# A gated linear attention with a maxout expert on one Trainium2 core: engine orders written out operation by operation, steps skewed by one tile, and the q and k products split over two engines

## The chip, the cores and the metric

The kernel runs on one core of a Trainium2 chip. The metric is the device time of one execution in microseconds (us); lower is better. A profiled execution also gives a span, from its first to its last instruction, and a trace of every engine: PE (TensorE; PEld is its weight loads), DVE (VectorE), ACT (ScalarE), POOL (GpSimd) and SP (SyncE, which issues all the transfers here).

## What is computed

Per batch (4) and head (8) a state of 48 x 48 is carried along 768 positions, decayed by a sigmoid gate; its output, with the heads side by side, goes through a maxout expert.

```python
f = 1.0 / (1.0 + np.exp(-f_logit))
for t in range(S):
    state = f[:, :, t, :, None] * state + np.einsum('bhd,bhe->bhde', k[:, :, t], v[:, :, t])
    y[:, :, t] = np.einsum('bhd,bhde->bhe', q[:, :, t], state)
x = y.transpose(0, 2, 1, 3).reshape(B * S, H * D)       # 3072 x 384
out = np.maximum(x @ w1, x @ w2) @ w_out                # 384 -> 1024 -> 384
```

## The kernel before

The 768 positions are cut into 6 chunks of 128 and every chunk is taken for the 4 batches in turn: 24 tiles, tile i being chunk i // 4 of batch i % 4, with 128 positions on the partitions and 8 heads x 48 on the free axis. Since max(a, b) = b + relu(a - b), the expert is computed as x (w2 w_out) + relu(x (w1 - w2)) w_out: `wd` = w1 - w2 and `w2o` = w2 w_out are made once at the start (24 transposes `w2tp` and 24 matmuls `w2op`).

One tile goes through these steps, each named by the tile that it writes:

- load: `ft`, `kt`, `qt`, `vt`, 192 KB each, one DMA each on SP (L63).
- `e`, `ell` on ACT (L177, L178): the log of the gate, negated; `vb` on DVE (L184): v in bf16.
- `cum` on PE (L191, L193): its sums along the chunk, as a matmul with a triangle of ones, and four small matmuls for the sum of the whole chunk.
- `ei`, `ed`, `fl` on ACT (L199 to L201): the exponentials of these; `kp` = k times `ei` and `qp` = q times `ed` on POOL (L203, L205; `qp` of tile 0 on DVE).
- `tr` on PE (L214): eight transposes of `kp` and `qp`; `trs` on DVE (L218) takes them out of PSUM.
- `a` on PE (L229): the eight 128 x 128 products of q and k; `am` on DVE (L232) masks them.
- `sa` on PE (L244), `tmp` on DVE (L248), two `st` on POOL (L251): the new state, for the same batch's next chunk, four tiles later. The last chunk needs none.
- `y` on PE (L256, L261): eight matmuls with `am`, and four with the old state except in the first chunk; `x` on ACT (L264).
- `xtp` on PE (L271; three transposes) and `xT` on DVE (L273).
- `d` on PE, two halves of 12 matmuls (L150), `gT` on ACT, the relu, one for each half (L152); `o` on PE, 11 matmuls (L162), written as six and five; `ob` on DVE (L167); the store of 192 KB on SP (L169).

No scheduler reorders anything: each engine, SP too, runs its instructions in the order in which the program writes them. The order is one of whole steps. Tiles 0 and 1 go through the attention steps, then the weights are prepared, then tiles 2 to 5 are begun; from i = 2 a loop writes `s_cum(i+3)`, `s_y(i)`, `u_d(i-1, 0)`, `s_tr(i+2)`, `u_d(i-1, 1)`, `s_xT(i)`, `s_a(i+1)`, `u_o(i-1, ...)`, `s_ell(i+4)`, `s_v(i+4)`, `load(i+6)`. So a tile is begun four steps ahead of its `y`, and every engine finds the instructions of one step in that order. On SP the loads of tiles 0 and 1 come first, then all weights (six of 512 KB, two of 768 KB), then tiles 2 to 5; later each step has one store and four loads.

PSUM has three buffers for `cum`, `sa`, `y`, `tr` and `xtp` (tag "s"), three for `d`, `o` and the weights (tag "mm"), one for `a`.

Of the kernel before, what the change touches and what calls it, by code (L numbers as in the profile page):

```python
# [14 lines left out]

@with_exitstack
def kernel(
# [35 lines left out]
    ld = {}  # L55

    def load(i):
        c, b = divmod(i, B)
        sl = slice(c * C, (c + 1) * C)
        t = {}  # L60
        for name, src in (("f", f_logit), ("k", k), ("q", q), ("v", v)):
            t[name] = loads.tile([C, H, D], F32, name=f"{name}t", tag=f"{name}t")
            nc.sync.dma_start(out=t[name], in_=src[b, :, sl, :].rearrange("h p d -> p h d"))  # L63
        ld[i] = t

    w1_f = consts.tile([C, JG, d_ff], F32, name="w1_f")
    w2_f = consts.tile([C, JG, d_ff], F32, name="w2_f")
    wo_f = consts.tile([C, FG, dm], F32, name="wo_f")

    def load_w(dst, src, j, n=1):  # L70
        nc.sync.dma_start(out=dst[:, j:j + n, :],
                          in_=src[j * C:(j + n) * C, :].rearrange("(j p) x -> p j x", p=C))

    load(0)
    load(1)
    for j in range(JG):
        load_w(w2_f, moe_w2, j)
    for j in range(0, FG, 4):
        load_w(wo_f, moe_w_out, j, 4)
    for j in range(JG):  # L80
        load_w(w1_f, moe_w1, j)
    load(2)
    load(3)
    load(4)
    load(5)


# [9 lines left out]
    for t in ell_b:  # L97
        nc.vector.memset(t, 0.0)
    nc.vector.memset(ones_col, 1.0)
    make_upper_triangular(nc, ut, 1.0, diag=True)  # L100
    make_identity(nc, ident)
    for t in kp_b + qp_b:
        nc.vector.memset(t, 0.0)
    nc.vector.tensor_copy(mask, ut.unsqueeze(1).to_broadcast([C, H, C]))
    for b in range(B):
        for t in st_b[b]:
            nc.vector.memset(t, 0.0)


# [6 lines left out]
    def u_w2_cast(j):  # L116
        nc.vector.tensor_copy(w2_h[:, j, :], w2_f[:, j, :])

    def u_wo_cast(h):
        s = slice(h * 2, h * 2 + 2)  # L120
        nc.scalar.copy(wo[:, s, :], wo_f[:, s, :])

    def u_wd(j):
        nc.vector.tensor_sub(wd[:, j, :], w1_f[:, j, :], w2_f[:, j, :])

    def u_w2T(f):
        ps = ps_m.tile([C, JG, C], BF16, name="w2tp", tag="mm")
        for j in range(JG):
            nc.tensor.transpose(out=ps[:, j, :], in_=w2_h[:, j, f * C:(f + 1) * C], identity=ident)  # L129
        nc.vector.tensor_copy(w2T[:, f, :], ps.rearrange("p j c -> p (j c)"))  # L130

    def u_w2o(j):
# [4 lines left out]
        nc.scalar.copy(w2o[:, j, :], ps)  # L137


    st = {}  # L140

    def u_d(i, half):
        s = st[i]
        if half == 0:
            s["g"] = work.tile([C, FG, C], BF16, name="gT", tag="gT")
        ps = ps_m.tile([C, 4, C], F32, name="d", tag="mm")
        for n in range(4):
            f = half * 4 + n
            for j in range(JG):
                nc.tensor.matmul(out=ps[:, n, :], lhsT=wd[:, j, f * C:(f + 1) * C], rhs=s["xT"][:, j, :],  # L150
                                 start=(j == 0), stop=(j == JG - 1))
        nc.scalar.activation(s["g"][:, half * 4:half * 4 + 4, :], ps, AF.Relu)  # L152

    def u_o(i, half):
        s = st[i]
        if half == 0:
            s["o"] = ps_m.tile([C, dm], F32, name="o", tag="mm")
        mms = [(s["xT"][:, j, :], w2o[:, j, :]) for j in range(JG)]
        mms += [(s["g"][:, f, :], wo[:, f, :]) for f in range(FG)]
        cut = 6  # L160
        for n in (range(0, cut) if half == 0 else range(cut, len(mms))):
            nc.tensor.matmul(out=s["o"], lhsT=mms[n][0], rhs=mms[n][1],  # L162
                             start=(n == 0), stop=(n == len(mms) - 1))
        if half == 1:
            c, b = divmod(i, B)
            ob = work.tile([C, dm], F32, name="ob", tag="ob", bufs=5)
            nc.vector.tensor_copy(ob, s["o"])  # L167
            r0 = b * S + c * C
            nc.sync.dma_start(out=out[r0:r0 + C, :], in_=ob)  # L169
            del st[i]  # L170


    def s_ell(i):
        t = ld[i]
        e = work.tile([C, dm], F32, name="e", tag="e")
        ell = ell_b[i % 2]
        nc.scalar.activation(e, t["f"].rearrange("p h d -> p (h d)"), AF.Exp, scale=-1.0)  # L177
        nc.scalar.activation(ell[:, :, 0:D], e.rearrange("p (h d) -> p h d", h=H), AF.Ln, bias=1.0)  # L178
        st[i] = {"ell": ell}

    def s_v(i):
        t = ld[i]
        vb = work.tile([C, dm], BF16, name="vb", tag="vb", bufs=6)
        nc.vector.tensor_copy(vb, t["v"].rearrange("p h d -> p (h d)"))  # L184
        st[i]["v"] = vb

    def s_cum(i):
        s, t = st[i], ld[i]
        ell = s["ell"]
        ps = ps_s.tile([C, 512], F32, name="cum", tag="s")  # L190
        nc.tensor.matmul(out=ps[:, 0:dm], lhsT=ut, rhs=ell[:, :, 0:D], start=True, stop=True)  # L191
# [11 lines left out]
        nc.gpsimd.tensor_mul(kp[:, :, 0:D], t["k"], ei.rearrange("p (h d) -> p h d", h=H))  # L203
# [1 line left out]
        eng.tensor_mul(qp[:, :, 0:D], t["q"], ed.rearrange("p (h d) -> p h d", h=H))  # L205
        s.update(fl=fl, qp=qp, kp=kp)
        del ld[i]

    def s_tr(i):
# [7 lines left out]
        tr = work.tile([C, 2, NP, C], BF16, name="trs", tag="trs", bufs=3)  # L217
        nc.vector.tensor_copy(tr, ps)  # L218
        s["tr"] = tr

    def s_a(i):
# [10 lines left out]
        nc.vector.tensor_mul(am.rearrange("p o n c -> p (o n) c"),  # L232
                             ps.rearrange("p o n c -> p (o n) c"), mask)
        s["am"] = am

    def s_y(i):
# [3 lines left out]
        old, new = st_b[b][c % 2], st_b[b][(c + 1) % 2]  # L240
        if c < nch - 1:
            sa = ps_s.tile([C, NP, 2 * D], F32, name="sa", tag="s")
            for p in range(NP):
                nc.tensor.matmul(out=sa[:, p, :],  # L244
                                 lhsT=s["kp"][:, 2 * p:2 * p + 2, :].rearrange("p h d -> p (h d)"),
                                 rhs=vb[:, 2 * p * D:(2 * p + 2) * D], start=True, stop=True)
            tmp = work.tile([C, NP, 2 * D], F32, name="tmp", tag="tmp")
            nc.vector.tensor_add(tmp, sa, old)  # L248
            for o in range(2):
                r, e = slice(o * DP, (o + 1) * DP), slice(o * D, (o + 1) * D)  # L250
                nc.gpsimd.tensor_mul(new[r, :, e], tmp[r, :, e],  # L251
                                     s["fl"][r, :].unsqueeze(2).to_broadcast([DP, NP, D]))
        y = ps_s.tile([C, dm], F32, name="y", tag="s")
# [9 lines left out]
        x = work.tile([C, dm], BF16, name="x", tag="x")  # L263
        nc.scalar.copy(x, y)  # L264
        s["x"] = x

    def s_xT(i):
        s = st[i]
        ps = ps_s.tile([C, JG, C], BF16, name="xtp", tag="s")
        for j in range(JG):  # L270
            nc.tensor.transpose(out=ps[:, j, :], in_=s["x"][:, j * C:(j + 1) * C], identity=ident)  # L271
# [102 lines left out]
```

## Time and profile before

| | us |
|---|---|
| median of 3 runs | 160.34 |
| lowest, highest | 160.21, 161.01 |
| the profiled execution | 159.27 |
| its span, first to last instruction | 157.5 |

The profiled execution took 1.77 us more than its span. Its page lists, for every engine, the time in which it was busy and its share of the span; a strip in 40 slices of 3.94 us, each digit the busy tenths of one slice; and groups of instructions by line of the kernel, with the mean duration of one in ns and the idle time of the engine in front of them. The chain of waits follows the end back through whatever released each step. A timeline row gives the start and the duration of an instruction or of a run of like ones, and in brackets how long its engine had been idle and for what.

### The profile page before, as it was taken

What the parts mean: (1) busy time and instruction counts of PE and PEld (TensorE: products, weight loads), DVE (VectorE), ACT (ScalarE), POOL (GpSimd) and SP (SyncE); (2) the same over time, 40 slices, a digit from 0 to 9 for tenths busy, and PEclk for the clock granted to TensorE, in tenths of its full rate; (3) what the DMA queues carried; (4) which work ended last, traced back from release to release, by engine and by line L of the source; (5) the groups of instructions that cost most, each with busy time, mean ns of one, the idle gap of its engine ahead of it and who ended that gap; (6) DMA issues with size and microseconds to landing.
All of it is one profiled execution on the core that took longest, in us unless ns stands there. A gap on an engine that the chain in (4) does not pass through costs nothing.

```text
span 157.5 us, 4506 instructions
## 1 busy us (share of the span) xinstructions
PE 133.0 (84%) x1816; PEld 103.2 (66%) x1816; DVE 98.0 (62%) x175; ACT 86.8 (55%) x200; POOL 66.9 (43%) x95
## 2 busy tenths in 40 slices
PE   0253559647699999999999999999999999999991
PEld 0131346336388777887788877887788777887770
DVE  7561669415356877676876676967676576754411
ACT  4406053547475757666586756757576656644330
POOL 2205220044484557654675447744576447400000
PEclk9999999977999999999999999999999999999998
DMA  5999999999099999699999799899989893111111
GB/s 104 198 248 387 396 342 172 189 190 174 2 199 186 228 194 224 133 230 200 205 212 194 174 205 226 174 233 207 237 186 229 178 219 81 50 54 50 54 50 50
DMA packets 105236, 28.60 MB, mean 182 GB/s; under 512 B 100352, under 2 KB 104448, under 8 KB 105216
## 3 DMA queue, kind: packets, MB, share of 16 engines
q1 hardware_dynamic: 105216, 28.32, 84.5%
q8 instruction: 14, 0.23, 0.6%
q14 instruction: 6, 0.05, 0.1%
HBM read 23.59 MB, written 4.72 MB: 180 GB/s over the span
## 4 chain that ended last, share of the span: by engine, by line
PE 69%; issue 7%; DMA 6%; POOL 5%; DVE 4%; ACT 4%; SPq 2%; POOLq 0%; ACTq 0%
PE o L162 25%; PE d L150 17%; PE tr L214 6%; DMA vt<-in_v_dram 6%; PE a L229 4%; PE w2op L135 3%; PE y L261 3%; PE xtp L271 3%; POOL qp L205 2%; SPq L63 2%; PE cum L191 2%; PE sa L244 2%; PE y L256 2%; POOL kp L203 2%; PE w2tp L129 2%
## 5 line engine op out<-in xcount | busy, mean ns | idle before, releaser
L203 POOL TENSOR_TENSOR kp<-kt,ei 128x384 bf16<-128x384 f32 x24 | 24.0, 999 | 57.7 <-issue 31.7
L150 PE MATMUL d<-xT,wd 128*128 128x128 bf16 x576 | 40.1, 221 | 0.0
L152 ACT ACTIVATE gT<-d 128x512 bf16<-128x512 f32 x48 | 29.5, 614 | 15.0 <-PE d L150 15.0
L162 PE MATMUL o<-wo,gT 128*128 128x384 bf16 x192 | 35.3, 326 | 0.0
L150 PEld LDWEIGHTS <-wd 128*128 128x128 bf16 x576 | 33.9, 99 | 0.2
L232 DVE TENSOR_TENSOR am<-a,mask 128x1024 bf16<-128x1024 f32 x24 | 29.3, 1222 | 1.3 <-PE a L229 1.3
L218 DVE COPY trs<-tr 128x1024 bf16<-128x1024 bf16 x24 | 16.5, 688 | 19.7 <-PE tr L214 19.7
L162 PEld LDWEIGHTS <-gT 128*128 128x128 bf16 x192 | 18.7, 98 | 12.3
L199 ACT ACTIVATE ei<-cum 128x384 f32<-128x384 f32 x24 | 11.8, 490 | 25.2 <-PE cum L193 23.8
L251 POOL TENSOR_TENSOR st<-tmp,fl 64x192 bf16<-64x192 f32 x40 | 20.0, 501 | 11.5 <-DVE tmp L248 10.0
L167 DVE COPY ob<-o 128x384 f32<-128x384 f32 x24 | 13.4, 558 | 18.2 <-PE o L162 18.2
L205 POOL TENSOR_TENSOR qp<-qt,ed 128x384 bf16<-128x384 f32 x23 | 23.4, 1018 | 0.0
L264 ACT CAST x<-y 128x384 bf16<-128x384 f32 x24 | 11.9, 496 | 18.8 <-PE y L261 18.8
L162 PE MATMUL o<-w2o,xT 128*128 128x384 bf16 x72 | 15.8, 329 | 0.0
L184 DVE CAST vb<-vt 128x384 bf16<-128x384 f32 x24 | 10.6, 443 | 7.9 <-DMA vt<-in_v_dram 7.8
L191 PE MATMUL cum<-ell,ut 128*128 128x384 bf16 x24 | 8.3, 347 | 8.0 <-ACT ell L178 8.0
L214 PE MATMUL tr<-ident,kp 128*128 128x128 bf16 x96 | 9.9, 229 | 5.9 <-POOL kp L203 5.7
L261 PE MATMUL y<-vb,am 128*128 128x48 bf16 x192 | 11.5, 186 | 2.8 <-DVE am L232 2.8
L177 ACT ACTIVATE e<-ft 128x384 f32<-128x384 f32 x24 | 12.5, 519 | 1.6 <-DMA ft<-in_f_logit_dram 1.6
L273 DVE COPY xT<-xtp 128x384 bf16<-128x384 bf16 x24 | 8.5, 355 | 7.4 <-PE xtp L271 5.1
L178 ACT ACTIVATE ell<-e 128x384 bf16<-128x384 f32 x24 | 12.5, 523 | 0.8
L193 PEld LDWEIGHTS <-ell 128*128 128x128 bf16 x96 | 6.1, 99 | 10.2 <-issue 7.7
(43 smaller groups left out, 164.8 us busy)
## 6 DMA issues: line engine op xcount, KB each, us to landing
ft<-in_f_logit_dram SPq DMA_DIRECT2D x24, 192.0 KB, 3.9
kt<-in_k_dram SPq DMA_DIRECT2D x24, 192.0 KB, 4.5
qt<-in_q_dram SPq DMA_DIRECT2D x24, 192.0 KB, 4.6
vt<-in_v_dram SPq DMA_DIRECT2D x24, 192.0 KB, 4.4
out_dram<-ob SPq DMA_DIRECT2D x24, 192.0 KB, 3.3
w_f<-in_moe_w_dram SPq DMA_DIRECT2D x6, 512.0 KB, 8.3
wo_f<-in_moe_w_out_dram SPq DMA_DIRECT2D x2, 768.0 KB, 8.9
```

The source lines that it names most:

```text
L150: nc.tensor.matmul(out=ps[:, n, :], lhsT=wd[:, j, f * C:(f + 1) * C], rhs=s["xT"][:, j, :], start=(j == 0), stop=(j == JG - 1))
L152: nc.scalar.activation(s["g"][:, half * 4:half * 4 + 4, :], ps, AF.Relu)
L162: nc.tensor.matmul(out=s["o"], lhsT=mms[n][0], rhs=mms[n][1], start=(n == 0), stop=(n == len(mms) - 1))
L167: nc.vector.tensor_copy(ob, s["o"])
L177: nc.scalar.activation(e, t["f"].rearrange("p h d -> p (h d)"), AF.Exp, scale=-1.0)
L203: nc.gpsimd.tensor_mul(kp[:, :, 0:D], t["k"], ei.rearrange("p (h d) -> p h d", h=H))
L205: eng.tensor_mul(qp[:, :, 0:D], t["q"], ed.rearrange("p (h d) -> p h d", h=H))
L214: nc.tensor.transpose(out=ps[:, n, p, :], in_=src[:, 2 * p:2 * p + 2, :].rearrange("p h d -> p (h d)"), identity=ident)
L218: nc.vector.tensor_copy(tr, ps)
L232: nc.vector.tensor_mul(am.rearrange("p o n c -> p (o n) c"), ps.rearrange("p o n c -> p (o n) c"), mask)
L251: nc.gpsimd.tensor_mul(new[r, :, e], tmp[r, :, e], s["fl"][r, :].unsqueeze(2).to_broadcast([DP, NP, D]))
L261: nc.tensor.matmul(out=y[:, ds], lhsT=am[:, o, p, :], rhs=vb[:, ds], start=(c == 0), stop=(c == 0 or o == 1))
```

## The change

The steps are taken apart into operations of one engine each (`a_e`, `a_ln`, `p_cum`, `a_ei`, ..., `v_ob`, `store`), and two tables of words are the whole program: PROLOGUE, run once, and STEP, run for i = 1 to 29. A word pair such as `kpv 1` runs the operation on tile i + 1, unless that tile had it already. Single lines of the two tables:

```diff
+PROLOGUE = """
...
+lv 0  lf 0  lf 1  lq 0  lk 0  lk 1  lq 1  lv 1  lw2 0  lw2 1  lwo 0  lw2 2  lwo 1  lw1 0
...
+STEP = """
+lk 5  lf 7  e 1  lq 5  ln 1  cum 1  d0 -1  ed 1  fl 1  ei 1  g0 -1  a 0  am 0  v 1  d1 -1
+g1 -1  kpv 1  lv 5  o0 -1  y 0  x 0  qp 1  sa 0  o1 -1  xT 0  tmp 0  st 0  tr 1  xTe 0  tre 1
+ob -1  out -1
```

The prologue brings tiles 0 and 1 to `ob`, tile 2 to `xT` and tile 3 to `trs`; so the first step with work on PE is i = 3. In a step i, `cum`, the products and `tr` belong to tile i + 1, `a`, `y`, `sa` and `xtp` to tile i, `d` and `o` to tile i - 1. A tile is thus begun one step ahead of its `y`.

```diff
+    def m_kp(i, eng):
+        s = st[i]
+        s["kp"] = kp_b[i % NQ]
+        eng.tensor_mul(s["kp"][:, :, 0:D], ld[i]["k"], s["ei"].rearrange("p (h d) -> p h d", h=H))
...
-        nc.gpsimd.tensor_mul(kp[:, :, 0:D], t["k"], ei.rearrange("p (h d) -> p h d", h=H))
-        eng = nc.vector if i < 1 else nc.gpsimd
-        eng.tensor_mul(qp[:, :, 0:D], t["q"], ed.rearrange("p (h d) -> p h d", h=H))
...
+    def warm(n):
+
+        ps = ps_m.tile([C, 512], F32, name="warm", tag="mm")
+        for _ in range(n):
+            nc.tensor.matmul(out=ps, lhsT=ell_b[1][:, 0:2, :].rearrange("p h d -> p (h d)"),
+                             rhs=ell_b[1].rearrange("p h d -> p (h d)"), start=True, stop=True)
...
+        "kp": lambda i: m_kp(i, nc.gpsimd), "kpv": lambda i: m_kp(i, nc.vector),
+        "qp": lambda i: m_qp(i, nc.gpsimd), "qpv": lambda i: m_qp(i, nc.vector),
...
+    def run(op, n):
+        key = (same.get(op, op), n)
+        if op == "warm" or key not in done:
+            done.add(key)
+            ops[op](n)
...
+    words = STEP.split()
+    for i in range(FIRST_STEP, T + 6):
+        for op, n in zip(words[0::2], words[1::2]):
+            if 0 <= i + int(n) < T:
+                run(op, i + int(n))
```

So in the loop `kp` is made on DVE and `qp` on POOL; for tiles 0 to 3 it is the other way round. New are 19 matmuls `warm` of 512 columns in the prologue, whose result nobody reads; `wd` of the first third on POOL (`wdp`); the cast of the first third of w2 on ACT (`w2ca`); and for tile 2 the transposes and their copy in two parts (`trk`, `trq`). The clearing of the eight state tiles goes from DVE to POOL. `gT` gets three buffers, `ob` six, `vb` five.

Three places, in the engines' own orders. DVE in one step of the loop, before (`vb` is of tile i + 4, `tmp` and `xT` of tile i, `trs` of tile i + 2, `am` of tile i + 1, `ob` of tile i - 1):

```order
L184 CAST vb<-vt 128x384
L248 TENSOR_TENSOR tmp<-sa,st_1_146 128x384
L218 COPY trs<-tr 128x1024
L273 COPY xT<-xtp 128x384
L232 TENSOR_TENSOR am<-a,mask 128x1024
L167 COPY ob<-o 128x384
```

and now (`am`, `tmp` and `xT` of tile i; `vb`, `kp` and `trs` of tile i + 1):

```order
L245 TENSOR_TENSOR am<-a,mask 128x1024
L184 CAST vb<-vt 128x384
L210 TENSOR_TENSOR kp_81<-kt,ei 128x8x48
L262 TENSOR_TENSOR tmp<-sa,st_1_89 128x384
L299 COPY xT<-xtp 128x384
L231 COPY trs<-tr 128x1024
L330 COPY ob<-o 128x384
```

DVE has seven instructions in a step instead of six, and `vb` and `kp` stand between `am` and `tmp`.

ACT in one step of the loop, before (`x` of tile i, `gT` of tile i - 1, `e` and `ell` of tile i + 4, `ei`, `ed` and `fl` of tile i + 3):

```order
L199 ACTIVATE ei<-cum 128x384
L200 ACTIVATE ed<-cum 128x384
L201 ACTIVATE fl<-cum 128x4
L264 CAST x<-y 128x384
L152 ACTIVATE gT<-d 128x512 x2
L177 ACTIVATE e<-ft 128x384
L178 ACTIVATE ell_144<-e 128x8x48
```

and now, from the `x` of one step to the `x` of the next (`e`, `ell` and the exponentials all of tile i + 1):

```order
L290 CAST x<-y 128x384
L176 ACTIVATE e<-ft 128x384
L180 ACTIVATE ell_85<-e 128x8x48
L201 ACTIVATE ed<-cum 128x384
L205 ACTIVATE fl<-cum 128x4
L197 ACTIVATE ei<-cum 128x384
L314 ACTIVATE gT<-d 128x512 x2
L290 CAST x<-y 128x384
```

The instructions are the same, but `e` and `ell` now stand right behind `x`, and the `cum` that opens the next step on PE needs them; before, they stood behind `gT`, and PE had the eleven matmuls of `o` in front of that `cum`.

SP behind the loads of tiles 0 and 1, before:

```order
L71 DMA w_f<-in_moe_w_dram 128x1024 x3
L71 DMA wo_f<-in_moe_w_out_dram 128x4x384 x2
L71 DMA w_f<-in_moe_w_dram 128x1024 x3
L63 DMA ft<-in_f_logit_dram 128x8x48
L63 DMA kt<-in_k_dram 128x8x48
L63 DMA qt<-in_q_dram 128x8x48
L63 DMA vt<-in_v_dram 128x8x48
```

and now:

```order
L134 DMA w_f<-in_moe_w_dram 128x1024 x2
L138 DMA wo_f<-in_moe_w_out_dram 128x4x384
L134 DMA w_f<-in_moe_w_dram 128x1024
L138 DMA wo_f<-in_moe_w_out_dram 128x4x384
L131 DMA w_f<-in_moe_w_dram 128x1024
L126 DMA qt<-in_q_dram 128x8x48
L131 DMA w_f<-in_moe_w_dram 128x1024 x2
L126 DMA ft<-in_f_logit_dram 128x8x48
L126 DMA vt<-in_v_dram 128x8x48
L126 DMA kt<-in_k_dram 128x8x48
```

The weights are as many and come at the same place but for one `qt`, that of tile 2, which now goes ahead of the last two thirds of w1 (L131). The next loads are `f` of tile 2, `v` of tile 3, `k` and `v` of tile 2, `f` and `k` of tile 3, `f` of tile 5, `q` of tile 3.

More of the change, by code (lines that the diff above doesn't have):

```diff
@@ L52 @@
     nc.scalar.preload_act_table_set("natural_log_exp_and_others")
[L55 to L85, printed above, removed]
     NQ = 4
@@ L96 @@
     mask = consts.tile([C, H, C], BF16, name="mask")
[L97 to L107, printed above, removed]
+    w1_f = consts.tile([C, JG, d_ff], F32, name="w1_f")
+    w2_f = consts.tile([C, JG, d_ff], F32, name="w2_f")
+    wo_f = consts.tile([C, FG, dm], F32, name="wo_f")
     w2_h = consts.tile([C, JG, d_ff], BF16, name="w2_h")
@@ L114, with setup @@
     w2o = consts.tile([C, JG, dm], BF16, name="w2o")
-    def u_w2_cast(j):
-        nc.vector.tensor_copy(w2_h[:, j, :], w2_f[:, j, :])
-    def u_wo_cast(h):
+    def setup(n):
+        if n == 0:
+            for t in ell_b:
+                nc.vector.memset(t, 0.0)
+            nc.vector.memset(ones_col, 1.0)
+            make_upper_triangular(nc, ut, 1.0, diag=True)
+            make_identity(nc, ident)
+            for t in (kp_b[0], qp_b[0]):
+                nc.vector.memset(t, 0.0)
+        elif n == 1:
+            nc.vector.tensor_copy(mask, ut.unsqueeze(1).to_broadcast([C, H, C]))
+            for t in kp_b[1:] + qp_b[1:]:
+                nc.vector.memset(t, 0.0)
+        else:
+            for b in range(B):
+                for t in st_b[b]:
+                    nc.gpsimd.memset(t, 0.0)
@@ new lines, with load, load_w1 @@
+    ld = {}
+    st = {}
+    SRC = {"f": f_logit, "k": k, "q": q, "v": v}
+    def load(i, names="fkqv"):
+        c, b = divmod(i, B)
+        sl = slice(c * C, (c + 1) * C)
+        for name in names:
+            t = loads.tile([C, H, D], F32, name=f"{name}t", tag=f"{name}t")
+            nc.sync.dma_start(out=t, in_=SRC[name][b, :, sl, :].rearrange("h p d -> p h d"))
+            ld.setdefault(i, {})[name] = t
+        st.setdefault(i, {})
+    def load_w1(j):
+        nc.sync.dma_start(out=w1_f[:, j, :], in_=moe_w1[j * C:(j + 1) * C, :])
@@ L136, in u_w2o @@
                              start=(f == 0), stop=(f == FG - 1))
[L137 to L170, printed above, removed]
@@ L173, in s_ell @@
[L173 to L190, printed above, removed]
+    def ev_w2o(j):
+        nc.scalar.copy(w2o[:, j, :], psum.pop(("w2o", j)))
+    def a_e(i):
+        e = st[i]["e"] = work.tile([C, dm], F32, name="e", tag="e")
+        nc.scalar.activation(e, ld[i]["f"].rearrange("p h d -> p (h d)"), AF.Exp, scale=-1.0)
+    def a_ln(i):
+        ell = st[i]["ell"] = ell_b[i % 2]
+        nc.scalar.activation(ell[:, :, 0:D], st[i]["e"].rearrange("p (h d) -> p h d", h=H), AF.Ln, bias=1.0)
@@ L191, in s_cum, with v_v, p_cum @@
+    def v_v(i):
+        vb = st[i]["v"] = work.tile([C, dm], BF16, name="vb", tag="vb", bufs=5)
+        nc.vector.tensor_copy(vb, ld[i]["v"].rearrange("p h d -> p (h d)"))
+    def p_cum(i):
+        ell = st[i]["ell"]
+        ps = psum["cum", i] = ps_s.tile([C, 512], F32, name="cum", tag="s")
         nc.tensor.matmul(out=ps[:, 0:dm], lhsT=ut, rhs=ell[:, :, 0:D], start=True, stop=True)
@@ L216, in s_tr, with v_tr, p_a @@
                                     identity=ident)
[L217 to L221, printed above, removed]
+    def v_tr(i, sel):
         s = st[i]
-        tr = s["tr"]
-        ps = ps_a.tile([C, 2, NP, C], F32, name="a", tag="a")
+        if "tr" not in s:
+            s["tr"] = work.tile([C, 2, NP, C], BF16, name="trs", tag="trs", bufs=3)
+        n = "kq".index(sel[0])
+        nc.vector.tensor_copy(s["tr"][:, n:n + len(sel)], psum.pop(("tr" + sel, i)))
+    def p_a(i):
+        tr = st[i]["tr"]
+        ps = psum["a", i] = ps_a.tile([C, 2, NP, C], F32, name="a", tag="a")
         for p in range(NP):
@@ L239, in s_y @@
         am, vb, tr = s["am"], s["v"], s["tr"]
[L240 to L253, printed above, removed]
+        old = st_b[b][c % 2]
+        y = psum["y", i] = ps_s.tile([C, dm], F32, name="y", tag="s")
         for p in range(NP):
@@ L262, in s_y @@
                                  start=(c == 0), stop=(c == 0 or o == 1))
[L263 to L267, printed above, removed]
-        s = st[i]
-        ps = ps_s.tile([C, JG, C], BF16, name="xtp", tag="s")
-        for j in range(JG):
-            nc.tensor.transpose(out=ps[:, j, :], in_=s["x"][:, j * C:(j + 1) * C], identity=ident)
-        s["xT"] = work.tile([C, JG, C], BF16, name="xT", tag="xT", bufs=5)
-        nc.vector.tensor_copy(s["xT"], ps)
@@ new lines, in p_xT, with v_xT, p_d @@
+    def p_xT(i):
+        ps = psum["xT", i] = ps_s.tile([C, JG, C], BF16, name="xtp", tag="s")
+        for j in range(JG):
+            nc.tensor.transpose(out=ps[:, j, :], in_=st[i]["x"][:, j * C:(j + 1) * C], identity=ident)
+    def v_xT(i):
+        t = st[i]["xT"] = work.tile([C, JG, C], BF16, name="xT", tag="xT", bufs=5)
+        nc.vector.tensor_copy(t, psum.pop(("xT", i)))
+    def p_d(i, half):
+        ps = psum["d", half, i] = ps_m.tile([C, 4, C], F32, name="d", tag="mm")
+        for n in range(4):
+            f = half * 4 + n
+            for j in range(JG):
+                nc.tensor.matmul(out=ps[:, n, :], lhsT=wd[:, j, f * C:(f + 1) * C], rhs=st[i]["xT"][:, j, :],
+                                 start=(j == 0), stop=(j == JG - 1))
@@ new lines, in a_g, with p_o @@
+    def a_g(i, half):
+        s = st[i]
+        if half == 0:
+            s["g"] = work.tile([C, FG, C], BF16, name="gT", tag="gT", bufs=3)
+        nc.scalar.activation(s["g"][:, half * 4:half * 4 + 4, :], psum.pop(("d", half, i)), AF.Relu)
+    def p_o(i, half):
+        s = st[i]
+        if half == 0:
+            psum["o", i] = ps_m.tile([C, dm], F32, name="o", tag="mm")
+        mms = [(s["xT"][:, j, :], w2o[:, j, :]) for j in range(JG)]
+        mms += [(lambda f=f: s["g"][:, f, :], wo[:, f, :]) for f in range(FG)]
+        cut = 6
+        for n in (range(0, cut) if half == 0 else range(cut, len(mms))):
+            l, r = mms[n]
+            nc.tensor.matmul(out=psum["o", i], lhsT=l() if callable(l) else l, rhs=r,
+                             start=(n == 0), stop=(n == len(mms) - 1))
@@ new lines, in v_ob, with store @@
+    def v_ob(i):
+        t = st[i]["ob"] = work.tile([C, dm], F32, name="ob", tag="ob", bufs=6)
+        nc.vector.tensor_copy(t, psum.pop(("o", i)))
+    def store(i):
+        c, b = divmod(i, B)
+        r0 = b * S + c * C
+        nc.sync.dma_start(out=out[r0:r0 + C, :], in_=st[i]["ob"])
+    def warm(n):
[3 more added lines that the diff above has]
+                             rhs=ell_b[1].rearrange("p h d -> p (h d)"), start=True, stop=True)
@@ new lines @@
+    same = {"kpv": "kp", "qpv": "qp", "w2ca": "w2c", "wdp": "wd", "trk": "tr", "trke": "tre"}
+    done = set()
+    def run(op, n):
[3 more added lines that the diff above has]
+            ops[op](n)
+    words = PROLOGUE.split()
+    for op, n in zip(words[0::2], words[1::2]):
+        run(op, int(n))
+    words = STEP.split()
+    for i in range(FIRST_STEP, T + 6):
+        for op, n in zip(words[0::2], words[1::2]):
+            if 0 <= i + int(n) < T:
+                run(op, i + int(n))
```

184 lines of the change are left out of this document (95 added, 89 removed).

## Prediction

> **What bounds the kernel now.** I read the page's busy times and strip first, for where PE has holes.
>
> ```profile
> PE 133.0 (84%) x1816; PEld 103.2 (66%) x1816; DVE 98.0 (62%) x175; ACT 86.8 (55%) x200; POOL 66.9 (43%) x95
> PE   0253559647699999999999999999999999999991
> ```
>
> PE is busy for 133 of 157.5 us, and the strip puts most of the missing 24.5 us into the first twelve slices, before 47 us. The busy times by stage say the same:
>
> ```profile
> 30.00:35.00 5.00, 1.39 (x13) 0.97 (x13) 0.36 (x1) 3.27 (x8) 1.95 (x2) 0.87 1.25 197
> 40.00:45.00 5.00, 3.77 (x51) 2.69 (x49) 2.07 (x4) 3.10 (x10) 2.61 (x3) 1.00 0.26 66
> 50.00:55.00 5.00, 5.00 (x79) 4.02 (x77) 4.36 (x8) 3.35 (x10) 3.05 (x5) 1.00 1.16 226
> ```
>
> The columns are busy us of PE, PEld, DVE, ACT and POOL, then clock, share of the transfers and GB/s. From 50 us on PE is never idle; from 30 to 35 us no engine is near its limit and PE has 1.39 us of work. Next, the chain of waits in one loop step:
>
> ```profile
> 59.22 0.67 PE d L150 x12
> 59.90 0.46 PE tr L214 x8
> 60.35 0.67 PE d L150 x12
> 61.02 0.17 PE xtp L271 x3
> 61.19 0.33 PE a L229 x8
> 61.52 1.89 PE o L162 x11
> 63.66 0.19 PE sa L244 x4
> 64.22 0.67 PE d L150 x12
> ```
>
> The chain never leaves PE. A step is 64.22 - 59.22 = 5.00 us and is the sum of its parts: two d 1.34, tr 0.46, xtp 0.17, a 0.33, o 1.89, cum 0.25 (from the end of o at 63.41 to sa), sa 0.19, y 0.37 (63.85 to 64.22). So the loop runs at PE's own pace and no other order of the same matmuls makes a step shorter; what can be won lies before 47 us. Of the transfers:
>
> ```profile
> 13.26 0.43 SPq L63 DMA_DIRECT2D ft<-in_f_logit_dram  x1
> 35.95 0.99 SPq L63 DMA_DIRECT2D vt<-in_v_dram  x1
> 42.68 0.36 SPq L169 DMA_DIRECT2D out_dram<-ob  x1
> 127.23 0.78 SPq L63 DMA_DIRECT2D vt<-in_v_dram  x1
> 32.18 0.36 DVE L184 CAST vb<-vt 128x384 bf16<-128x384 f32 x1 [2.99 <-DMA vt<-in_v_dram]
> 36.40 0.36 DVE L184 CAST vb<-vt 128x384 bf16<-128x384 f32 x1 [0.44 <-DMA vt<-in_v_dram]
> DMA to landing us min/median/max: 2.8/3.9/11.5
> ```
>
> Here vb of tiles 3 and 4 waited for their loads: these landed 4.22 us apart, so one load of 192 KB takes 1.05 us when they are dense. From 42.68 to 128.01 SP issued 18 stores and 72 loads: 4.74 us a tile, of which the store is 4.74 - 4 x 1.05 = 0.54. The transfers thus run just below PE's pace of 5.00. SP stood still from 36.94 to 42.68, until the first ob was there.
>
> **When the weights are there.** The last row is ft's: the longest load of the gate, which I take for the one issued at 13.26 behind the weights, landed at 24.8, so the last of w1 had landed by about 23.8. In the new order q of tile 2 goes ahead of it: 24.8.
>
> **Part 1, the prologue, to the start of step 3.** The prologue needs wd in full before its first d. Three subtractions took 3.49 us on DVE:
>
> ```profile
> 25.44 3.49 DVE L124 TENSOR_TENSOR wd<-w_f 128x1024 bf16<-128x1024 f32 x3
> 30.91 0.53 ACT ell L178
> 31.49 0.32 PE cum L191
> ```
>
> so one, 1.16 us behind the landing, gives 26.0 for the first d. (The chain's other two rows: cum follows 0.05 us behind ell; I use 0.05 for a hand-over.) Behind it PE has in the prologue four halves of d 2.68, two o 3.78, two tr 0.92, two cum 0.50, a 0.33, sa 0.19, y 0.37, xtp 0.17: 8.9 us. On top come three places where the written order makes PE wait: o of tile 0 for a gT that stands behind the three exponentials on ACT (0.5), a of tile 2 for the copy of the transposes just in front of it (0.4), xtp of tile 2 for x (0.4). That makes 36.2. The data allow it: v of tile 3 was the eighth load behind the weights and landed at 32.1; q of tile 3 is the ninth (q of tile 2 counted), 33.2, and behind it lie only a product of 0.55, tr 0.46, xtp 0.17 and half of o 0.86: 35.2. Without the waits it is 34.9; with the waits doubled and loads 0.5 late, 38.0.
>
> The other new pieces of the prologue cost nothing that I can find. The 19 warm matmuls lie where PE waits for loads or products; at 384 columns an o matmul takes 1.89 / 11 = 0.17 us, so all 19, of 512 columns, are an estimated 4.4 us, spread over 20 us in which PE would be idle. Were they on the path they would cost that; and a gain from them in the matmuls before 26 us would be worth nothing, as the weights' landing comes last. wdp on POOL handles 1024 columns; by the row of kp below, 999 ns for 384, that is 2.66 us, or 1.16 if it were as fast as on DVE; it may start when the first of w1 is there, about 4 us before the last, so it is done in time either way. Clearing the eight states is 1.7 us on DVE:
>
> ```profile
> L107 DVE MEMSET st<- 128x192 uint32 x8 | 1.7, 218 | 0.0
> ```
>
> On POOL it is between that and, at the ratio of the products below (999 to 551), 3.2 us; it stands ahead of kp of tile 0, whose tile is done long before 26.0.
>
> **Part 2, the steps.** From step 3 the work on PE is 17 steps of 5.00 (i = 3 to 19), three without sa of 4.81, one without cum, tr and sa of 4.10, and d and o of the last tile, 3.23: 106.8 us. Whether PE gets through without waiting depends on two chains that the new order makes short.
>
> ```profile
> 11.40 0.50 PE L261 MATMUL y<-vb,am 128*128 128x48 bf16 x8 [0.89 <-DVE am L232]
> 11.94 0.48 ACT L264 CAST x<-y 128x384 bf16<-128x384 f32 x1 [5.63 <-PE y L261]
> 61.55 0.52 ACT L177 ACTIVATE e<-ft 128x384 f32<-128x384 f32 x1
> 62.10 0.52 ACT L178 ACTIVATE ell<-e 128x384 bf16<-128x384 f32 x1
> 64.56 0.50 ACT L264 CAST x<-y 128x384 bf16<-128x384 f32 x1
> 64.93 0.64 ACT L152 ACTIVATE gT<-d 128x512 bf16<-128x512 f32 x1
> ```
>
> First, ACT: y, x, e, ell, cum. x starts 0.04 behind y's end; y's last matmul ends about 0.15 behind the start of PE's next work (63.85 + 0.37 = 64.22 against the first d matmul's issue, an estimate from how the rows overlap); the next instruction starts 0.37 behind x (64.56 to 64.93), ell 0.55 behind e, lasts 0.52, and 0.05 to cum: 0.15 + 0.04 + 0.37 + 0.55 + 0.52 + 0.05 = 1.68 us. Meanwhile PE has sa 0.19, five o matmuls 0.86, xtp 0.17 and tr 0.46: 1.68. It is just even; I put 0.05 us a step on it, 20 x 0.05 = 1.0 us, with 0 and 0.3 as the ends.
>
> ```profile
> L205 DVE TENSOR_TENSOR qp<-qt,ed 128x384 bf16<-128x384 f32 x1 | 0.6, 551 | 0.0
> L203 POOL TENSOR_TENSOR kp<-kt,ei 128x384 bf16<-128x384 f32 x24 | 24.0, 999 | 57.7 <-issue 31.7
> L232 DVE TENSOR_TENSOR am<-a,mask 128x1024 bf16<-128x1024 f32 x24 | 29.3, 1222 | 1.3 <-PE a L229 1.3
> L218 DVE COPY trs<-tr 128x1024 bf16<-128x1024 bf16 x24 | 16.5, 688 | 19.7 <-PE tr L214 19.7
> ```
>
> Second, DVE: it was busy 98.0 / 24 = 4.1 us a tile; kp adds 0.55 (the one product that DVE did): 4.65 of 5.00, and less on the wall, as its rows overlap. In order: am follows a, then vb and kp, tmp behind sa, xT behind xtp, trs behind tr, ob. trs ends about 0.15 + 0.69 us behind PE's next start and must be there for the next a, which cum 0.25 and d 0.67 separate from tr: even again, with some 0.1 to spare. So 0.55 us more on DVE is hidden, but only by the time between kp and tmp. POOL loses 24 us in all and has 2 us of work a step.
>
> Loads: from q of tile 3 (33.2) to q of tile 6 SP has 13 loads and a store, 33.2 + 13 x 1.05 + 0.54 = 47.4; POOL could use it at step 5, about 36.2 + 2 x 5.05 + 1 = 47.3, and tr of tile 6 is due 3.4 us later. That is the tightest: 2.3 us to spare behind a product of 1.0. Afterwards loads gain 0.3 us a step. So they are hidden, and cost if not is the second rival.
>
> **Part 3, the end.** In the last steps xT of a tile is wanted by the very next d.
>
> ```profile
> 144.81 0.33 PE L271 MATMUL xtp<-ident,x 128*128 128x128 bf16 x3
> 145.18 0.36 DVE L273 COPY xT<-xtp 128x384 bf16<-128x384 bf16 x1 [1.32 <-PE xtp L271]
> 152.37 1.80 PE o L162 x11
> 154.20 0.56 DVE ob L167
> ```
>
> From xtp's issue end (144.81 + 0.17) to the copy's end and a hand-over is 0.6 us, in full for tile 23, and 0.15 for tile 22, whose tr covers the rest: 0.75. From the last o to the end of the span it stays at 157.5 - 154.2 = 3.3 us.
>
> **Sum.** 36.2 + 106.8 + 1.0 + 0.75 + 3.3 = 148.05 us of span. The profiled execution took 159.27 for a span of 157.5, 1.77 more: 149.8. The median of the runs lay 160.34 - 159.27 = 1.07 above the profiled one: 150.9 us, 9.4 us less than before.
>
> **The rivals.** *ACT sets the pace.* If the in-order queue lets x start later (in the loop before it started 0.34 behind y's end, as fl was in front of it), each cum waits 0.3 us: 20 x 0.25 more, 155.9. For it: the chain is even to 0.01. Against: in the new order nothing stands in front of x but gT, done 0.5 us earlier.
>
> *Loads come late.* Before, dense loads have rows of 1.05 us; a tenth more would put q of tile 6 near 49.6 us, with its product 0.1 from the time of its tr, and every later delay would pass to PE through vb and kp at the head of DVE's queue. I put it at 3 us: 153.9. Against: 72 loads went at 4.74 a tile.
>
> *DVE and POOL collide, and it is slower.* In the profile a cast that starts beside a product on POOL lasts until that is over:
>
> ```profile
> 99.35 1.00 POOL L203 TENSOR_TENSOR kp<-kt,ei 128x384 bf16<-128x384 f32 x1 [2.00 <-issue]
> 99.36 1.20 DVE L184 CAST vb<-vt 128x384 bf16<-128x384 f32 x1 [0.38 <-DMA vt<-in_v_dram]
> ```
>
> 1.20 us where 0.36 do, as in the rows above. If in every step vb and kp on DVE met qp or st on POOL, they would lose 0.85 and up to 1.0 us; tmp, xT and trs would follow, and the d that needs xT would start some 0.95 late: 20 x 0.95 = 19 us, 170. It turns the sign from 0.47 us a step (9.4 / 20). Against: qp starts behind ed, while PE has the first d, and is over about 0.7 us before am lets vb go; st starts only behind tmp. It decides only if q lands so late that qp slips by that much.
>
> The Trainium skill, "SBUF — State Buffer", section "Who interferes with whom", names this case: a VectorE instruction with two inputs in SBUF contends with a GpSimd instruction that reads SBUF, and the second to issue blocks fully; kp on DVE is such a one. The cast's row agrees with a full block; no run here shows the two-input form beside POOL. By that rule qp on DVE beside kp on POOL in the prologue (tiles 2 and 3) would add an estimated 0.3 to 0.5 us, and the sum would be 151.3; in the loop it changes nothing as long as qp is early.
>
> *The prologue gains less*: PE starts step 3 at 40 instead of 36.2, if ACT, which takes e of tile 2 ahead of the first gT, waits longer for that load: 154.7.
>
> *Nothing is gained*: the transfers bound the end anyway. Against: their pace of 4.74 a tile would bring the last v at about 126 us, and from its cast some 13 us of work are left: 139.
>
> **How the numbers follow.** The forecast, 149 to 152.5, has 0.50; better by 2 to 3 us (no waits in the prologue) 0.05; ACT's pace 0.15, late loads 0.12, a shorter gain in the prologue 0.08; no change for a reason that I don't see 0.03; slower by the collision or another wait of half a microsecond in each step 0.07. A measurement of this kernel can tell about 0.5% from no change, 0.8 us. Faster: 0.90, within 0.03, slower 0.07. The range, 147.3 to 157.0, takes in prologue starts from 34.9 to 38.0, waits per step from 0 to 0.3, and the first three rivals that stay faster; it leaves out 0.10 and a little of the tails.
>
> **What would show it.** Right: PE full from about 26 us, step 3's cum at 36, steps of 5.05 us on average, PE's last o 3.3 us ahead of the end, kp on DVE near 0.55 us with POOL idle beside it. Wrong: steps of 5.3 with cum waiting for ell (ACT's pace); vb or kp waiting for vt or kt after 45 us (loads); vb or kp of over 0.8 us in most steps (collision); a first d after 29 us (the prologue).

## The result, and the profile after

| | before | after | after, measured again | predicted |
|---|---|---|---|---|
| median, us | 160.28 | 150.99 | 150.84 | 150.9 |
| ratio to before, 95% interval | | 0.9464 (0.9365 to 0.9563) | 0.9428 (0.9381 to 0.9475) | 0.941 |
| profiled execution, us | 159.27 | 150.64 | 150.91 | 149.8 |
| its span, us | 157.5 | 148.9 | 149.1 | 148.05 |

The change takes 9.3 us off the median. By the ratio the kernel is 5.4% faster, with an interval of 4.4 to 6.4%; the executions come in two states, and the ratio compares those in the faster one, which leaves out one of the four of the kernel before (161.01 us). The page of the changed kernel, its busy times and strip:

```profile
PE 134.7 (90%) x1835; PEld 101.6 (68%) x1835; DVE 107.4 (72%) x189; ACT 89.5 (60%) x201; POOL 50.7 (34%) x81
PE   0369879899999999999999999999999999999981
```

PE's busy time is 1.7 us longer, with the warm matmuls in it; of the holes before 47 us, those behind 30 us are gone, and the earlier ones are smaller, partly by warm matmuls. The busy times by stage, with the columns as before, say where:

```profile
25.00:30.00 5.00, 4.39 (x54) 3.19 (x53) 1.99 (x2) 3.85 (x10) 0.99 (x1) 1.00 0.95 175
30.00:35.00 5.00, 4.86 (x67) 3.50 (x65) 4.29 (x9) 3.12 (x9) 0.99 (x1) 1.00 1.38 194
50.00:55.00 5.00, 5.00 (x76) 3.95 (x75) 3.94 (x8) 3.36 (x9) 2.00 (x3) 1.00 0.94 188
```

From 30 to 35 us PE has 4.86 us of work instead of 1.39; in the loop it is as full as before. The chain of waits shows where step 3 begins, some later steps, the first of the three steps without sa, and the end:

```profile
36.19 0.16 PE cum L189
...
41.00 0.27 PE cum L189
...
96.98 0.27 PE cum L189
...
102.07 0.27 PE cum L189
...
122.43 0.27 PE cum L189
...
125.96 0.48 ACT x L290
126.44 0.43 ACT e L176
126.89 0.53 ACT ell L180
127.47 0.32 PE cum L189
...
137.53 0.83 PE d L307 x12
...
143.77 1.80 PE o L325 x11
```

Step 3 begins at 36.2 in the chain, which counts its cum from the end of the o in front of it; the timeline has that cum issued at 36.02. From step 4 (41.00) to step 20 (122.43) there are 16 steps of 81.43 / 16 = 5.09 us; before, a step was 5.00. From step 3 to PE's last o the chain leaves PE only three times: in steps 20 and 21 for x, e and ell (125.96 and 131.05), and at 141.85 for xT of the last tile. The gain is the earlier start; the steps themselves are 0.09 us worse. One of them in the timeline, on ACT and PE:

```profile
95.79 0.53 ACT L176 ACTIVATE e<-ft 128x384 f32<-128x384 f32 x1
96.35 0.52 ACT L180 ACTIVATE ell<-e 128x384 bf16<-128x384 f32 x1
96.59 0.39 PE L222 MATMUL tr<-ident,qp 128*128 128x128 bf16 x4
96.93 0.32 PE L189 MATMUL cum<-ell,ut 128*128 128x384 bf16 x1
```

Four transposes are issued in 0.22 us (in this step those of kp at 96.37, those of qp at 96.59), so cum could go at 96.81; ell ends at 96.87 and cum is issued at 96.93. The wait is 0.1 us, too short for a bracket, since the last transposes are still on their way through PE.

### The profile page after: what moved, and what is told of

Read it like the earlier page. It is cut to its first block, busy times and chain, and to the rows that moved or that the text cites. A ratio compares the mean times of both kernels' runs of the same rounds, so it can differ in the third digit from the quotient of the medians.

```text
span 148.9 us, 4490 instructions
## 1 busy us (share of the span) xinstructions
PE 134.7 (90%) x1835; PEld 101.6 (68%) x1835; DVE 107.4 (72%) x189; ACT 89.5 (60%) x201; POOL 50.7 (34%) x81
## 4 chain that ended last, share of the span: by engine, by line
PE 72%; ACT 2%; DVE 1%; issue 0%
PE o L325 26%; PE d L307 22%; PE tr L222 6%; PE a L240 5%; PE cum L189 4%; PE y L285 3%; PE y L280 2%; PE xtp L295 2%; PE sa L254 2%; PE cum L191 1%; ACT ell L180 1%; ACT x L290 1%; ACT e L176 1%; DVE ob L330 0%; DVE qp L215 0%; DVE xT L299 0%
## 5 line engine op out<-in xcount | busy, mean ns | idle before, releaser
L325 PE MATMUL o<-wo,gT 128*128 128x384 bf16 x192 | 38.9, 326 | 0.4 <-ACT gT L314 0.4
L314 ACT ACTIVATE gT<-d 128x512 bf16<-128x512 f32 x48 | 29.0, 607 | 10.2 <-PE d L307 10.1
L307 PEld LDWEIGHTS <-wd 128*128 128x128 bf16 x576 | 32.6, 97 | 3.4 <-issue 0.6
L215 POOL TENSOR_TENSOR qp<-qt,ed 128x384 bf16<-128x384 f32 x20 | 20.0, 998 | 21.1 <-POOL st L269 10.9
L325 PEld LDWEIGHTS <-gT 128*128 128x128 bf16 x192 | 17.3, 98 | 10.1 <-ACT gT L314 0.8
L231 DVE COPY trs<-tr 128x1024 bf16<-128x1024 bf16 (+1 forms) x25 | 16.6, 669 | 4.5 <-PE tr L222 2.7
L201 ACT ACTIVATE ed<-cum 128x384 f32<-128x384 f32 x24 | 11.7, 489 | 11.2 <-POOL st L269 9.1
L262 DVE TENSOR_TENSOR tmp<-sa,st 128x384 f32<-128x384 f32 x20 | 11.1, 556 | 6.4 <-issue 6.4
L285 PEld LDWEIGHTS <-am 128*128 128x128 bf16 x192 | 9.6, 96 | 2.3 <-DVE am L245 0.7
```

The source lines that it names most:

```text
L215: eng.tensor_mul(s["qp"][:, :, 0:D], ld[i]["q"], s["ed"].rearrange("p (h d) -> p h d", h=H))
L231: nc.vector.tensor_copy(s["tr"][:, n:n + len(sel)], psum.pop(("tr" + sel, i)))
L285: nc.tensor.matmul(out=y[:, ds], lhsT=am[:, o, p, :], rhs=vb[:, ds], start=(c == 0), stop=(c == 0 or o == 1))
L325: nc.tensor.matmul(out=psum["o", i], lhsT=l() if callable(l) else l, rhs=r, start=(n == 0), stop=(n == len(mms) - 1))
```

## The experiments

Every kernel was timed beside the kernel before on the same chip; where a step starts and how long it is, is read from the issue of cum in the timeline of one trace (36.02 for step 3 of the changed kernel). Words that are left out of a line of the tables are marked with three dots. The runs ask first whether it is the prologue or the steps, then what holds the steps, then what the pieces are worth.

**The old prologue in front of the new steps.** The prologue's table is rewritten in the order of the kernel before, with its loads and casts and without the warm matmuls; the steps stay.

```diff
-lv 0  lf 0  lf 1  lq 0  lk 0  lk 1  lq 1  lv 1  lw2 0  lw2 1  lwo 0  lw2 2  lwo 1  lw1 0
...
+lf 0  lk 0  lq 0  lv 0  lf 1  lk 1  lq 1  lv 1  lw2 0  lw2 1  lw2 2  lwo 0  lwo 1  lw1 0  lw1 1
...
+wd 0  wd 1  wd 2  e 2  ln 2  v 2  cum 2  ei 2  ed 2  fl 2  kp 2  qp 2  e 3  ln 3  v 3  tr 2  tre 2
+d0 0  g0 0  cum 3  ei 3  ed 3  fl 3  kp 3  qp 3  a 2  am 2  d1 0  g1 0  tr 3  tre 3  o0 0  o1 0
```

> The steps of the changed kernel behind a prologue in the order of the kernel before (whole steps: tiles 0 and 1, then the weights, then tiles 2 and 3; no warm matmuls, casts and wd where they were, loads in the old order). Theory (all of the gain is the prologue's): step 3 begins at 46 to 48.5 us, steps of 5.09, span 159 to 161.5, so no faster than before or a little slower. Rival (skew and split carry a good part of it): span below 156.

Measured: 160.86 us, ratio 1.0097 (1.0040 to 1.0153), span 159.9; step 3 begins at 47.1, steps of 5.09. The whole gain is gone, and the new steps alone are a little slower than the old kernel. Its stages show one thing that no theory had (clock in the third column from the right):

```profile
30.00:35.00 5.00, 1.94 (x18) 1.52 (x18) 0.65 (x2) 2.53 (x7) 2.14 (x2) 0.74 1.31 198
35.00:40.00 5.00, 4.66 (x44) 3.71 (x43) 1.92 (x3) 2.03 (x5) 1.95 (x2) 0.50 1.12 148
40.00:45.00 5.00, 5.00 (x40) 3.17 (x39) 0.95 (x2) 1.19 (x2) 0.00 (x0) 0.73 0.11 32
```

Behind the idle stretch the granted clock is 0.50, and half a d takes 1.49 us instead of 0.83.

**The same with warm matmuls in the gap**, to part the order from the clock.

```diff
-wd 0  wd 1  wd 2  e 2  ln 2  v 2  cum 2  ei 2  ed 2  ...
+warm 6  wd 0  wd 1  wd 2  e 2  ln 2  v 2  cum 2  warm 9  ei 2  ed 2  ...
```

> As old_prologue, with six warm matmuls behind the products of the weights and nine behind cum of tile 2, where PE stood idle before its granted clock fell to 0.50. Theory (the old prologue loses to both, its order and the low clock from 33 to 43 us that its idle time brings): step 3 begins 3 to 4.5 us earlier, at 42.5 to 44, still 6 us or more behind the new prologue; span 155.5 to 157. Rival (PE waits for ACT and loads there in any case): step 3 within 1 us of 47, span above 158.5.

Measured: 159.38 us, ratio 0.9967 (0.9930 to 1.0004), span 157.9; the clock is 1.00 throughout, step 3 begins at 45.1. So 2.0 us of the old prologue's loss was the clock, between the two expectations of 3 to 4.5 and of less than 1; what is left, 9 us to 36.02, is put down to its order. The 2.0 us are rather too low: cum of tile 2 came 0.79 us later in this execution (31.54 against 30.75), behind products of the weights that took 5.31 us instead of 4.51, and from there to step 3 the saving is 2.8 us. Part of what a full clock could save went into longer waits for kp and qp (0.54, 0.79 and 0.56 us; in the run before they were 0.34, none and 0.34); from its timeline:

```profile
34.67 0.40 PE L219 MATMUL tr<-ident,qp 128*128 128x128 bf16 x4 [0.54 <-POOL qp L212]
37.88 0.40 PE L219 MATMUL tr<-ident,kp 128*128 128x128 bf16 x4 [0.79 <-POOL kp L207]
38.83 0.40 PE L219 MATMUL tr<-ident,qp 128*128 128x128 bf16 x4 [0.56 <-POOL qp L212]
```

**The new prologue in front of the old steps.** With the old order kp is back on POOL in the steps, beside qp.

```diff
-lk 5  lf 7  e 1  lq 5  ln 1  cum 1  d0 -1  ed 1  fl 1  ei 1  g0 -1  a 0  am 0  v 1  d1 -1
-g1 -1  kpv 1  lv 5  o0 -1  y 0  x 0  qp 1  sa 0  o1 -1  xT 0  tmp 0  st 0  tr 1  xTe 0  tre 1
-ob -1  out -1
+cum 3  ei 3  ed 3  fl 3  kp 3  qp 3  sa 0  tmp 0  st 0  y 0  x 0  d0 -1  g0 -1  tr 2  tre 2
+d1 -1  g1 -1  xT 0  xTe 0  a 1  am 1  o0 -1  o1 -1  ob -1  out -1  e 4  ln 4  v 4
+lf 6  lk 6  lq 6  lv 6
...
-FIRST_STEP = 1
+FIRST_STEP = 0
```

> The prologue of the changed kernel, then steps in the order of the kernel before (cum of tile i + 3, tr of i + 2, a of i + 1, e and vb of i + 4, kp and qp on POOL). Theory (the skew of one tile matters only at the start, where loads come just in time: the old skew needs f of tile 6 and kp and qp of tiles 4 and 5 before y of tile 3): y of tile 3 near 43 us instead of 39, then steps of 5.00, span 150 to 153. Rival (the skew does not matter, only the prologue): y of tile 3 at 39 to 40 and span near 147.

Measured: 155.74 us, ratio 0.9735 (0.9680 to 0.9789), span 153.7. The steps are 5.00 us, as before, but in front of y of tile 3 PE stands still twice: cum of tile 5 waits for an ell that ACT makes behind the exponentials of tile 4, and cum of tile 6, which now stands ahead of that y, waits for its load; from its timeline:

```profile
38.49 0.32 PE L189 MATMUL cum<-ell,ut 128*128 128x384 bf16 x1 [2.05 <-ACT ell L180]
42.19 0.52 ACT L176 ACTIVATE e<-ft 128x384 f32<-128x384 f32 x1 [2.26 <-DMA ft<-in_f_logit_dram]
43.32 0.48 PE L189 MATMUL cum<-ell,ut 128*128 128x384 bf16 x1 [3.31 <-ACT ell L180]
```

After it the clock is down again (0.54 from 40 to 45 us) and the next cum starts 6.8 us later, at 50.09; then all is even. So with this order of loads the early prologue needs the short skew: loads come just in time, and a tile begun four steps ahead asks for its loads too soon. Whether the old steps would do with the gate's loads moved forward, as in a later run here, was not tried. The mechanism held, with y of tile 3 at 44.0; the span came 0.7 us above the expected range, which had not reckoned with the clock. Alone, then, the new prologue brought 2.65% and the new steps nothing; the 5.4% need both.

**e and ell one step earlier**, at the same place on ACT, to take them off the way from x to cum.

```diff
-lk 5  lf 7  e 1  lq 5  ln 1  cum 1  d0 -1  ed 1  fl 1  ei 1  g0 -1  a 0  am 0  v 1  d1 -1
+lk 5  lf 7  e 2  lq 5  ln 2  cum 1  d0 -1  ed 1  fl 1  ei 1  g0 -1  a 0  am 0  v 1  d1 -1
```

> The changed kernel, but in the steps e and ell are made for tile i + 2 instead of i + 1, at the same place on ACT; so cum finds its ell made one step earlier. Theory (ACT's chain x, e, ell, cum holds every step by 0.09 us and the three steps without sa by about 0.2): steps of 5.00 us instead of 5.09, 4.81 without sa, the span 2.0 us shorter, near 146.9, the time near 149. Rival (the 0.09 us are PE's own, from the change to matmuls over 48 rows between the two halves of d): steps stay at 5.09 and the span at 148.9.

Measured: 151.78 us, ratio 0.9529 (0.9479 to 0.9579), span 150.2. The steps became 4.98 us, 4.81 without sa, as the theory has it, and yet the kernel got no faster: two steps took 6.4 and 6.5 us. In both ACT stood behind a load, as its timeline has it (start, duration, and in brackets the idle time and what ended it):

```profile
43.05 0.52 ACT L176 ACTIVATE e<-ft 128x384 f32<-128x384 f32 x1 [2.44 <-DMA ft<-in_f_logit_dram]
49.58 0.52 ACT L176 ACTIVATE e<-ft 128x384 f32<-128x384 f32 x1 [2.54 <-DMA ft<-in_f_logit_dram]
```

Both e are in front of the exponentials that the same step needs, so the whole step waited for a gate that only the next one wanted.

**The same, with the gate's loads moved forward.**

```diff
-lv 4  lk 5  lq 5  e 0  ln 0  lv 5  ...
+lv 4  lf 6  lk 5  lq 5  e 0  ln 0  lv 5  ...
...
-...  v 3  lf 6  d1 1  g1 1  lk 6  lv 6  o0 1
-kp 3  qpv 3  lk 7  sa 2  ...  lq 6  o1 1
-ob 1  lf 7  lq 7
+...  v 3  lf 7  d1 1  g1 1  lk 6  lv 6  o0 1
+kp 3  qpv 3  lq 6  lf 8  lk 7  sa 2  ...  o1 1
+ob 1  lq 7
```

> As e_ahead (e and ell one step earlier), with the loads of the gate moved forward to match: f of tile 6 ahead of k of tile 5, f of tile 7 right behind the first store, f of tile 8 ahead of k of tile 7, q of tile 6 ahead of them. Theory (in e_ahead the two steps of 6.4 and 6.5 us were ACT waiting for f of tiles 6 and 7, and the rest ran at 4.98): all steps at 5.00 or below, span 146.0 to 147.0, time near 148.5. Rival (the transfers as a whole are short by that much, so another load is then late): a step of over 5.5 us appears at k, v or q of tiles 6 to 8, span above 148.5.

Measured: 148.64 us, ratio 0.9284 (0.9245 to 0.9324), span 146.8, against 150.84 us, ratio 0.9428 (0.9381 to 0.9475), of the changed kernel in the same session; the intervals don't touch. All steps from step 4 to step 20 are 4.98 us. This version beats both kernels, and settles what the 0.09 us were: ACT's chain, not PE's own order, which by itself takes 4.98; the chain cost 0.11 a step.

**kp back on POOL in the steps.**

```diff
-g1 -1  kpv 1  lv 5  ...
+g1 -1  kp 1  lv 5  ...
```

> The changed kernel, but kp in the steps is back on POOL, in front of qp. Theory (the split is not needed for the pace): kp starts behind ei, qp is over about 0.8 us before its first transpose; vb waits up to 1.2 us for POOL, which is hidden; steps within 0.05 us of 5.09, span within 1 us of 148.9. Rival (the split is what makes a skew of one tile possible): tr waits for qp in every step, steps of 5.4 us or more, span of 155 or more.

Measured: 150.98 us, ratio 0.9481 (0.9410 to 0.9553), span 149.2, steps of 5.09. The steps don't change; what does was expected, and is hidden. From its groups by line (busy us, then the mean in ns):

```profile
L184 DVE CAST vb<-vt 128x384 bf16<-128x384 f32 x24 | 22.8, 950 | 0.1
```

vb takes 950 ns instead of 360, as it now meets kp and qp on POOL, and no step notices. So the split over two engines in the steps, by itself, is not worth anything that this measurement can tell.

**Without the warm matmuls.**

```diff
-lv 4  ...  cum 0  ei 0  ed 0  fl 0  warm 3
+lv 4  ...  cum 0  ei 0  ed 0  fl 0  ...
...
-...  w2T 4  w2Te 4  woc 0  warm 1  wd 1  w2o 1  w2oe 1  w2o 0
+...  w2T 4  w2Te 4  woc 0  wd 1  w2o 1  w2oe 1  w2o 0
```

> The changed kernel without its 19 warm matmuls. Theory as predicted (the landing of w1 sets the first d, so faster matmuls before it are worth nothing): first d within 0.2 us of 26.1, span within 0.5 us of 148.9. Rival (the products of the weights end at the same moment as wd, so PE's speed before 26 us counts): w2op takes 5.0 us or more instead of 4.3 and the transposes before it more too, first d 1 to 2.5 us later, span 150 to 151.5.

Measured: 151.49 us, ratio 0.9514 (0.9453 to 0.9575), span 149.6; step 3 begins at 36.78, 0.76 us later, and the steps are the same. In medians this can't be told from no change, and the 0.76 us are one pair of traces: in the five other traces with the warm matmuls of this prologue the same cum, of tile 4, was issued between 36.04 and 36.72. In its timeline the mechanism can be seen:

```profile
21.89 5.16 PE L166 MATMUL w2op<-wo,w2T 128*128 128x384 bf16 x24
26.88 1.50 PE L306 MATMUL d<-xT,wd 128*128 128x128 bf16 x24
```

w2op takes 5.16 us instead of 4.2, and the first d starts at 26.88 instead of 26.11. In this run the last wd was done at 25.56, so d waited for w2op alone; in all six traces with those warm matmuls it was the last wd that d waited for. It is the rival's mechanism, at less than its price. PE was slower well before that, too: sa of tile 1 took 0.50 us here and 0.34 in the changed kernel, though the clock column reads 1.00 for both from 15 to 20 us.

**The changed kernel once more.**

> The changed kernel once more, beside the others on the same chip: span 148.8 to 149.7, steps of 5.09 us from step 4 on. If the steps or their first start (36.0) come out otherwise, differences below 1 us between the other runs mean nothing.

Measured: 150.84 us, span 149.1, step 3 at 36.3, steps of 5.08 to 5.09.

## Why the prediction was right, point by point

- **What bounds the kernel** (PE in the loop, the prologue ahead of it): right. The old prologue in front of the new steps is as slow as the kernel before. That the new prologue gains its full worth only with the short skew was not part of it.
- **The prologue** (step 3 at 36.2): 36.19. The first d, with wd in full, was put at 26.0. Two of its matmuls started at 26.11, but the others at 26.59, since the last of w1 was there at 25.31, not 24.8. Of the three waits, 1.3 us in all, the one for gT was there with 0.40; the others were not, but tr of tile 3 waited 0.3 us for its product. So PE was 0.6 us later at the start and 0.6 us quicker behind it; that the sum is right is luck by that much.
- **"Worth nothing"** (what a faster PE does before 26 us): wrong, by 0.8 us in one pair of traces. The step took the landing of w1 as the only thing in front of the first d; the products of the weights end at nearly the same moment. From the changed kernel's timeline:

```profile
24.81 1.46 PE L167 MATMUL w2op<-wo,w2T 128*128 128x384 bf16 x8
25.31 1.22 DVE L152 TENSOR_TENSOR wd<-w_f 128x1024 bf16<-128x1024 f32 x1 [0.68 <-DMA w_f<-in_moe_w_dram]
26.59 1.40 PE L307 MATMUL d<-xT,wd 128*128 128x128 bf16 x22 [0.20 <-DVE wd L152]
```

  w2op ends at 26.27, wd at 26.53: whichever is made later moves the start. With the warm matmuls the landing does come last, as the step says; without them w2op does.
- **The steps** (106.8 + 1.0 + 0.75, to PE's end at 144.75): PE's last o ended at 145.57, 0.8 us later. The mechanism was right and named, ACT's chain against PE's work behind y, 1.68 to 1.68; its size was put at 0.05 a step and measured 0.09 beside the 5.00 of before, or 0.6 us over 16 steps. Missed was that in the three steps without sa PE has 0.19 us less to do while the chain is as long: the sum gave them 4.81 + 0.05, they took (137.53 - 122.43) / 3 = 5.03, 0.5 us in all. Step 3 gave 0.2 back: its y, of the first chunk, has no matmuls with the old state.
- **From the profiled time to the median**: 1.07 us was added, as before the change; it was 0.35. This error and the 0.8 us of span missed in the sum cancel; that the median is right to 0.1 us is luck in that measure.
- **DVE takes kp and hides it**: right. kp took 0.55 us as the one row of before said; DVE was busy 107.4 / 24 = 4.5 us a tile, and stood idle some 0.2 us ahead of am in most steps. Its group in the changed kernel:

```profile
L210 DVE TENSOR_TENSOR kp<-kt,ei 128x384 bf16<-128x384 f32 x20 | 11.0, 550 | 0.0
```

- **Loads hidden**: right, with as little to spare as was reckoned: q of tile 6, put at 47.4, landed at 47.65, and its product on POOL started at 47.81. vb never waited. But taking the gate one step earlier, in the first experiment on e, cost two waits of 2.5 us.
- **The rivals.** *ACT sets the pace*: it does, at 0.09 us a step instead of 0.3. *Loads come late*: not in this order. *DVE and POOL collide*: the block is real, its place was not in the loop. In the prologue qp of tile 2 on DVE met kp on POOL, in the changed kernel's timeline:

```profile
28.90 0.99 POOL L210 TENSOR_TENSOR kp<-kt,ei 128x384 bf16<-128x384 f32 x1 [5.35 <-ACT ei L197]
29.23 1.07 DVE L215 TENSOR_TENSOR qp<-qt,ed 128x384 bf16<-128x384 f32 x1 [2.70 <-ACT ed L201]
```

  It ended at 30.30 instead of 29.78, 0.41 behind the end of kp, and nothing waited, since PE was at the o of tile 0 until 30.31. The Trainium skill, "SBUF — State Buffer", section "Who interferes with whom", has it that a VectorE instruction with two inputs in SBUF blocks against a GpSimd one that reads SBUF; these rows agree, 1.07 us instead of 0.55. For tile 3 it was vb that met kp, and there PE did wait:

```profile
33.08 0.99 POOL L210 TENSOR_TENSOR kp<-kt,ei 128x384 bf16<-128x384 f32 x1 [3.19 <-ACT ei L197]
33.65 0.64 DVE L184 CAST vb<-vt 128x384 bf16<-128x384 f32 x1
34.21 0.55 DVE L215 TENSOR_TENSOR qp<-qt,ed 128x384 bf16<-128x384 f32 x1
34.81 0.23 PEld L222 LDWEIGHTS <-qp 128*128 128x128 bf16 x4 [0.31 <-DVE qp L215]
```

  vb took 0.64 us instead of 0.35, qp stood behind it, and the transposes of qp waited 0.31. So the collision in the prologue cost some 0.3 us of PE's time, as these rows read; no run parts it. That is the lower end of the 0.3 to 0.5 put down for it, though not by qp itself.

## What to carry to other kernels

Where PE is full in the loop, a new order can only win where PE is not full yet: look at the strip for the holes, and count what the first full step needs, load by load. A short skew between the engines lets the loop start on the first tiles that have landed, but it puts every engine's own order on the path: add up what stands between two operations of the critical engine on each other engine, and do so for the shorter steps too. Taking an operation out of that path a step earlier is worth it only with its load moved as well, since an in-order engine that waits for next step's load also holds up this step's work.

## What was not expected of the hardware

Idle time costs twice. Behind a stretch in which PE had 1.94 us of work in 5, its granted clock was 0.50 for 5 us and 0.73 for the next 5, and the fifteen matmuls that filled the stretch brought step 3 forward by 2.0 us. The kernel before has it too. The prediction's row has 0.87 from 30 to 35 us; the next five read:

```profile
35.00:40.00 5.00, 3.91 (x49) 3.22 (x47) 2.28 (x3) 2.84 (x7) 1.96 (x2) 0.79 1.11 156
```

The mean clock of its executions was 0.966 to 0.987, that of the changed kernel 0.996 to 1.000. So a part of the 9.3 us is the clock's: in the profiled execution at most 1.7 us, an estimate from the shares that the clock lost in these ten us (0.13 and 0.21 of 5 us each). No run parts it from the order in the kernel before, and the prediction did not reckon with it.

A copy on DVE can stand behind a whole row of POOL instructions. The clearing of the states moved to POOL, and the copy of the mask beside it took 3.09 us, where 0.36 did before. From the changed kernel's timeline:

```profile
1.75 2.93 POOL L113 MEMSET st<- 128x384 bf16 x8
1.88 3.09 DVE L107 COPY mask<-ut 128x1024 bf16<-128x1024 bf16 x1
```

It ended 0.29 us behind the eighth clearing, not behind the first, and it took 3.09 us in all nine traces that have the clearing on POOL. So, as these rows read, back-to-back work on one of the two kept the other out for all of it. Nothing needed the mask by then.
